# Sink-window attention with a two-layer block: in the start-up, the next pair's first row maxima ahead of VectorE's copies, and chunk 0's last pair ahead of pair 4's third scores

## The chip, the cores and the metric

One NeuronCore of a Trainium2 chip. The metric is the device time of one execution in microseconds; the times below come from a few executions of the kernel, and one more execution was recorded by the hardware profiler. Engines are named as in the profile: PE (TensorE matrix products), PEld (its weight loads), DVE (VectorE), ACT (ScalarE), POOL (GpSimd), SP (the queue that issues nearly all transfers).

## The reference

Attention over 4 batches, 8 heads, 768 positions, head size 64; each query sees the first 4 positions and the 128 last ones. Then, over all 3072 tokens, a block of two matrices with a squared ReLU between them.

```
scores = q @ k.T / 8                      # (4, 8, 768, 768)
keep   = (pos_k < n_sink) | ((0 <= pos_q - pos_k) & (pos_q - pos_k < window))
a      = softmax(where(keep, scores, -1e9))
x      = (a @ v), heads side by side      # (3072, 512)
h      = maximum(x @ w_in, 0)             # (3072, 2048)
out    = (h * h) @ w_out                  # (3072, 512)
```

The weights arrive as doubles; the kernel itself splits each row of 512 of them into two numbers (a "row" below: 16 of w_in, 16 of w_out).

## The kernel before

**Units of work.** The tokens are cut into 8 chunks of 384 (three blocks of 128 queries); the heads go in pairs, four pairs to a chunk. `pairs[s]` is pair s: pairs 0 to 3 are chunk 0, pairs 4 to 7 chunk 1. For a pair, in this order:

- `scores(s, i)`: for both heads, the product of query block i with its keys (PE, L254), the mask and row maximum (DVE, L262), the exponential with its row sum (ACT, L265). In chunk 0 block 0 is narrow (128 keys), the others have 264.
- `normalise(s)`: DVE adds a small number to the sums (L278) and takes reciprocals (L279); POOL multiplies the probabilities by them (L290) and gathers the sink columns in `PSK` (L296, L297).
- `tail(s)`: PE transposes the probabilities (`probs`, L344), three banks, and the sink columns (`sink_keys`, L304). Bank 0 and 2 are copied to `PTF` by ACT (L351), bank 1 by DVE (L349); DVE copies the sinks to `SK` (L310, L311). (For chunk 1 ACT makes all of these.)
- `values(s)`: PE multiplies by the values (L392, L395); ACT copies the result to `xh` (L403), DVE makes the rest `xl` (L404).

**Rows.** `split_steps` handles a row in five steps, and `fill(n)` issues the next n steps: (1) ACT copy L554 into tile `m`, DVE L555 into `t1`; (2) DVE L557; (3) DVE L559 into the other half words of `m`; (4) DVE L561; (5) ACT cast L567, DVE product L568, which reads `m`. There is one buffer for `m`.

**Order.** Up to the end of chunk 0's first products every engine runs in the order of the program text (`manual_schedule`), so an instruction that waits holds up all behind it on its engine. For s = 0 to 4 the loop issues: the load of pair s+1, scores(s, 0..2) with steps 1 to 3 of a row between them, step 4, normalise(s), values(s-2), the load of v, tail(s-1) with the rest of values(s-2), and step 5 inside it. Behind the loop: values(3), two steps, then the products of chunk 0 (`ph`, L451: x times w_in, and `po`, L488: the squares times w_out) in quanta; between them come two row steps and one entry of `todo` (scores, normalise, tail and values of pairs 4 to 7). ACT applies ReLU and a square (L459, L462), DVE the products L469 and L473. Later chunks and rows follow in an order that a planner spreads over the products.

Tiles of scores and of transposes share PSUM banks: three pairs of banks (`att`, `h`, `o0`/`o1`) rotate from pair to pair, so a product may start only when the bank's previous content was copied out. Dummy products (`busy`, L623) keep PE running in the first 16 us.

Of the kernel before, what the change touches and what calls it, by code (L numbers as in the profile page):

```python
# [19 lines left out]
P = 128  # L20
# [22 lines left out]
def sink_window_attention_moe(  # L43
# [25 lines left out]
    with ExitStack() as fast:  # L69
# [226 lines left out]
                nc.gpsimd.tensor_copy(to[:, :, 0:3:2, own], src.unsqueeze(2).broadcast_to([P, NQ - i0, 2, NS]))  # L296
                nc.gpsimd.tensor_tensor(to[:, :, 1, own], src, f32(to[:, :, 0, own]), op=ALU.subtract)  # L297

        def sink_keys(c, p, tag="att"):
            n = NQ - (1 if c % NHALF == 0 else 0)  # L300
            pss = bank(tag, f"pss_{c}_{p}")
            own = PSK[p % 2 if c < 2 else 0]
            for a in range(0, n, 2):
                nc.tensor.transpose(  # L304
                    pss[:, a * SW : a * SW + P], f32(own[:, a : a + 2]).rearrange("p a c -> p (a c)"), ident
                )
            copy = nc.scalar.copy if c == 1 else nc.vector.tensor_copy
            blocks = lambda t: t.rearrange("p (a c) -> p a c", c=P)
            rows = slice(0, 6 * NS)
            copy(blocks(SK[rows, 0 : n * P])[:, 0:n:2], blocks(pss[rows, 0 : (n + 1) // 2 * P]))  # L310
            copy(SK[rows, P : 2 * P], pss[SW : SW + 6 * NS, 0:P])  # L311

        def banks_of(c, p):

# [13 lines left out]
                banks.append((blocks, off))  # L328
            return banks

        def probs(c, p, bi, tag="att"):
            st = state[c, p]
            half = c % NHALF
            if bi == 0:
                st["banks"] = banks_of(c, p)
                st["PT"] = {}
            blocks, used = st["banks"][bi]
            pt = bank(tag, f"pt_{c}_{p}_{bi}")
            for hh, kk, qs, off in blocks:
                kb = st["kb0"] + kk  # L340
                for j, i in enumerate(qs):
                    qb = half * NQ + i
                    c0 = 0 if (qb == 0 or qb == kb + 1) else BS
                    nc.tensor.transpose(  # L344
                        pt[:, off + j * P : off + (j + 1) * P], st["P"][hh][:, i, c0 : c0 + P], ident
                    )
            st["PT"][bi] = PTF = ap3.tile([P, 512], F32, tag="PTF", name=f"PTF_{c}_{p}_{bi}")
            if bi == 1 and c != 1:
                nc.vector.tensor_copy(PTF[:, 0:used], pt[:, 0:used])  # L349
            else:  # L350
                nc.scalar.copy(PTF[:, 0:used], pt[:, 0:used])  # L351

        def probs_of(c, p, hh):

# [190 lines left out]
        def split_steps(n):  # L545
# [5 lines left out]
            m = ap1.tile([P, WR], I32, tag="m", name=f"m_{n}")  # L551
            eb = ap1.tile([P, WR], I32, tag="eb", name=f"eb_{n}")
            m16 = m.bitcast(U16).rearrange("p (w t) -> p w t", t=2)
            nc.scalar.copy(m16[:, :, 0], words[:, :, 1])  # L554
            nc.vector.tensor_scalar(t1, top, 3, 0x3FFFF000, op0=ALU.logical_shift_left, op1=ALU.bitwise_and)  # L555
            yield
            nc.vector.scalar_tensor_tensor(t1, top, -0x40000000, t1, op0=ALU.bitwise_and, op1=ALU.bitwise_or)  # L557
            yield
            nc.vector.tensor_scalar(m16[:, :, 1], words[:, :, 2], 0x1FF, None, op0=ALU.bitwise_and)  # L559
            yield  # L560
            nc.vector.tensor_scalar(eb, t1, -0x800000, None, op0=ALU.bitwise_and)  # L561
# [45 lines left out]
        with tc.manual_schedule(engines={E.PE, E.DVE, E.Activation, E.Pool, E.SP}):  # L607
# [7 lines left out]
            def scores(s, i, tags=("att", "att"), heads=(0, 1)):  # L615
                for hh in heads:
                    score(*pairs[s], hh, i, tags[hh])
# [4 lines left out]
                for _ in range(n):  # L622
                    nc.tensor.matmul(t, idle[:, 0:P], idle, start=True, stop=True)  # L623

            def tail(s, spare, own=("att",) * 3):

                a = pairs[s]
                probs(*a, 0, own[0])
                if s == 0:
                    busy(10)  # L630
                yield
                sink_keys(*a, spare)
                probs(*a, 1, own[1])
                yield
                probs(*a, 2, own[2])
                yield

            load_qk(*pairs[0])
# [8 lines left out]


            trio = [("att", "att"), ("h", "h"), ("o0", "o1")]
            for s in range(NPAIR + 1):  # L650
                if s > 0:
                    load_qk(*pairs[s + 1])
                trios = trio[-s % 3 :] + trio[: -s % 3]
                if s == 0:

                    for i, tags in enumerate(trios):
                        scores(s, i, tags, (0,))
                for i, tags in enumerate(trios):
                    scores(s, i, tags, (0, 1) if s else (1,))
                    if s == 0 or i > 0:  # L660
                        fill(1)
                fill(1)

                normalise(*pairs[s], (0, 1))
                if s == 1:
                    split_sinks()
                if s < 2:
                    busy(4 + 4 * s)
                rest = values(*pairs[s - 2], True) if s > 1 else None
                if s > 0:  # L670
                    if s > 1:
                        load_v(*pairs[s])
                    t = tail(s - 1, "o2", (*trios[0], trios[1][0]))
                    next(t)
                    fill(1)
                    if rest:
                        rest()
                    next(t)
                    fill(1)
                    next(t)  # L680
                else:
                    fill(1)
            rest = values(*pairs[NPAIR - 1], True)
            fill(2)
            rest()

            todo = []
            for s in range(NPAIR + 1, 2 * NPAIR + 1):
# [294 lines left out]
```

## Time and profile before

| | |
|---|---|
| time, median of 3 runs (lowest to highest) | 708.75 us (706.12 to 709.47) |
| the profiled execution | 708.04 us, of which the profile's span is 706.0 us |
| PE busy | 688.1 us, 97% of the span |
| DVE, ACT, POOL busy | 435.3 us, 428.6 us, 228.5 us |
| granted TensorE clock, mean | 0.995 |

The profiled execution's time is 2.0 us more than its span. Busy times are sums over the whole span; which engine sets the pace differs between the start-up (the first 41 us, where little is multiplied) and the rest.

### The profile page before, as it was taken

The page shows a single profiled execution, that of the slowest core. Times are in us where ns is not written, and L with a number is a line of the kernel's source. Part 1 is how long each engine was busy: PE and PEld are TensorE (multiplying, and loading weights), DVE is VectorE, ACT ScalarE, POOL GpSimd, SP SyncE. Part 2 cuts the span into 40 slices and gives each one's busy share as a digit, 9 for nine tenths or more (in the row PEclk, how much of TensorE's full clock was granted, in tenths as well). Part 3 has the DMA queues.
Part 4 walks back from the last instruction along what each step waited for, and adds up shares of the span by engine and source line. Part 5 has one row for each costly group of instructions (what it writes and reads, how often), then busy time and mean ns, then how long its engine had stood idle before and what let it go on. Part 6 is the DMA issues. An engine that isn't in the chain of part 4 may idle for free.

```text
span 706.0 us, 11716 instructions
## 1 busy us (share of the span) xinstructions
PE 688.1 (97%) x3865; PEld 594.5 (84%) x3866; DVE 435.3 (62%) x1181; ACT 428.6 (61%) x1200; POOL 228.5 (32%) x433
## 2 busy tenths in 40 slices
PE   9879999999999999999999999999999999999995
PEld 4557789998888898888888888889888889889995
DVE  7989899845667665565556566665555655542221
ACT  6777787755666676766676676667667444422221
POOL 5645400043455423323433443232344233200000
PEclk9999999999999999999999999999999999999999
DMA  7475466321524433333434532344432210000001
GB/s 239 149 234 185 131 213 204 130 65 42 149 70 125 122 109 92 92 101 107 102 105 113 152 87 73 102 128 108 101 93 84 88 44 16 0 16 31 1 0 50
DMA packets 37028, 71.51 MB, mean 101 GB/s; under 512 B 4384, under 2 KB 14368, under 8 KB 36960
## 3 DMA queue, kind: packets, MB, share of 16 engines
q1 hardware_dynamic: 36816, 70.55, 34.1%
q8 instruction: 33, 0.54, 0.3%
q14 instruction: 35, 0.29, 0.1%
q10 hardware_dynamic: 144, 0.13, 0.1%
HBM read 62.80 MB, written 7.86 MB: 100 GB/s over the span
## 4 chain that ended last, share of the span: by engine, by line
PE 90%; ACT 3%; DVE 3%; DMA 2%; issue 1%; SPq 0%; DVEq 0%; ACTq 0%
PE ph L451 37%; PE po L488 37%; PE xo L392 6%; PE s L258 5%; PE pt L362 2%; ACT P L265 2%; PE xo L395 2%; PE s L254 1%; DMA kn<-in_k_dram 1%; PE pt L344 1%; PE pss L304 1%; ACT m L554 1%; DMA ob<-part 1%; DMA part<-ob 0%; DVE P L262 0%
## 5 line engine op out<-in xcount | busy, mean ns | idle before, releaser
L451 PE MATMUL ph<-x,wi 128*128 128x384 f32 x1536 | 306.0, 340 | 0.0
L451 PEld LDWEIGHTS ph<-x,wi 128*128 128x128 f32 x1536 | 265.1, 188 | 8.9 <-issue 1.4
L488 PE MATMUL po<-wo,gh 128*128 128x512 f32 (+1 forms) x770 | 244.2, 398 | 1.0 <-DVE ob L512 0.8
L226 POOL TENSOR_TENSOR KS<-kn,KS 128x408 fp32r<-128x408 f32 (+1 forms) x48 | 59.0, 1229 | 318.4 <-ACT KS L225 318.4
L488 PEld LDWEIGHTS po<-wo,gh 128*128 128x128 f32 x770 | 135.8, 188 | 19.9 <-issue 1.4
L488 PE MATMUL po<-wo,gl 128*128 128x512 f32 x385 | 151.6, 394 | 0.0
L265 ACT ACTIVATE P<-P,nbs 128x264 f32<-128x264 f32 (+1 forms) x192 | 94.3, 492 | 78.5 <-DVE nbs L262 78.2
L459 ACT ACTIVATE r<-ph 128x384 f32<-128x384 f32 x128 | 62.3, 487 | 92.5 <-PE ph L451 89.8
L469 DVE TENSOR_TENSOR ph<-ph,r 128x384 f32<-128x384 f32 x104 | 58.4, 562 | 72.7 <-ACT r L459 72.6
L262 DVE CUSTOM_DVE_ANT_0 P<-s,masks 128x264 f32<-128x264 f32 x160 | 67.2, 429 | 56.3 <-PE s L258 53.5
L290 POOL TENSOR_SCALAR P<-P,rs 128x136 f32<-128x136 f32 (+2 forms) x192 | 83.9, 452 | 36.7 <-DVE rs L279 27.3
L473 DVE TENSOR_TENSOR gl<-ph,gh 128x384 fp32r<-128x384 f32 x128 | 71.2, 556 | 25.2 <-ACT ph L466 14.3
L488 PEld LDWEIGHTS po<-wo,gl 128*128 128x128 f32 x385 | 72.2, 188 | 16.0
L462 ACT ACTIVATE gh<-r 128x384 fp32r<-128x384 f32 x128 | 67.2, 525 | 3.0
L228 DVE TENSOR_TENSOR QS<-qn,QS 64x384 fp32r<-64x384 f32 x48 | 47.1, 982 | 25.6 <-ACT QS L227 25.2
L285 POOL TENSOR_TENSOR P<-P 128x256 f32<-128x256 f32 (+1 forms) x48 | 50.0, 1041 | 24.4 <-ACT P L265 23.9
L258 PE MATMUL s<-KS,QS 128*128 128x264 f32 (+1 forms) x288 | 57.0, 280 | 0.0
L258 PEld LDWEIGHTS s<-KS,QS 128*128 128x128 f32 x288 | 52.0, 188 | 5.0 <-DVE nbs L262 0.5
L368 DVE TENSOR_TENSOR PTF<-pt,halves 128x256 f32<-128x256 f32 x96 | 36.3, 419 | 22.3 <-PE pt L362 21.8
L392 PE MATMUL xo<-PTF,vn 128*64 128x256 f32 x448 | 47.3, 348 | 2.7 <-ACT PTF L351 2.7
L392 PEld LDWEIGHTS xo<-PTF,vn 128*64 128x64 f32 x448 | 32.1, 138 | 19.3 <-issue 9.2
L225 ACT CAST KS<-kn 128x408 fp32r<-128x408 f32 (+1 forms) x48 | 28.3, 589 | 32.1 <-issue 18.7
(99 smaller groups left out, 631.7 us busy)
## 6 DMA issues: line engine op xcount, KB each, us to landing
raw<-in_moe_w_in_dram SPq DMA_DIRECT2D x16, 512.0 KB, 3.9
raw<-in_moe_w_out_dram SPq DMA_DIRECT2D x16, 512.0 KB, 4.3
half<-in_moe_w_in_dram SPq DMA_DIRECT2D x32, 256.0 KB, 3.1
half<-in_moe_w_out_dram SPq DMA_DIRECT2D x32, 256.0 KB, 3.1
kn<-in_k_dram SPq DMA_DIRECT2D x24, 272.0 KB, 4.3
qn<-in_q_dram SPq DMA_DIRECT2D x32, 192.0 KB, 3.8
out_dram<-ob SPq DMA_DIRECT2D x23, 256.0 KB, 2.3
kn<-in_k_dram SPq DMA_DIRECT2D x24, 204.0 KB, 3.6
```

What stands on the lines that cost most here:

```text
L226: nc.gpsimd.tensor_tensor(KS[:, 1, 0:nk], st["kn"][:, hh, 0:nk], f32(KS[:, 0, 0:nk]), op=ALU.subtract)
L258: nc.tensor.matmul(ps[:, 0:n], st["QS", hh][:, qcols], flat[:, a, c0 : c0 + n], start=(a == 0), stop=(a == 1))
L262: nc.vector.tensor_tensor_reduce(Pt[:, i, 0:n], ps[:, 0:n], mask[:, 0:n], -SCALE, BIG, ALU.add, ALU.min, nb)
L265: nc.scalar.activation(Pt[:, i, 0:n], Pt[:, i, 0:n], AF.Exp, bias=nb, scale=-1.0, accum_out=sm[:, i : i + 1])
L290: nc.gpsimd.tensor_scalar(Pt[:, j, 0:n], Pt[:, j, 0:n], rs[:, hh, j : j + 1], 1.0, op0=ALU.mult, op1=ALU.mult)
L392: nc.tensor.matmul(xo[h * D : h * D + D, cols], lhsT, rhs, start=(n == 0), stop=False, skip_group_check=True)
L451: nc.tensor.matmul(ph[:, 0:TOK], wi_at(i, cc, fc), xt[:, cc, :], start=(m == 0), stop=(m == 3 * NCC - 1),)
L459: nc.scalar.activation(r, ph[:, 0:TOK], AF.Relu)
L462: nc.scalar.activation(gh, r, AF.Square)
L469: nc.vector.tensor_tensor(ph[:, 0:TOK], ph[:, 0:TOK], r, op=ALU.mult)
L473: late = lambda: nc.vector.tensor_tensor(gl, ph[:, 0:TOK], f32(gh), op=ALU.subtract)
L488: nc.tensor.matmul(po[t][:, e], gt[:, ts_], wo[f][:, i, e], start=(f == f0 and j == 0), stop=(f == f1 - 1 and j == 2), skip_group_check=True,)
```

## The change

Three edits, all in the order of instructions; no arithmetic changes.

1. The loop runs over s = 0 to 3. `scores(s+1, 0)` is issued in turn s, behind tail(s-1)'s PE work and step 4, and ahead of DVE's part of tail(s-1) (the copies to SK and to PTF) and of the rest of values(s-2). For that `sink_keys` and `probs` get a flag `later`, with which they return their DVE copies instead of issuing them.
2. Turn 4 is written out. In it, tail(3) goes ahead of scores(4, 2), and values(3) follows these scores, ahead of normalise(4). As many row steps are issued before the first product as before (27), with other places: one each after scores(4, 1), after the rest of values(2) and after normalise(4), and four at the end.
3. In `split_steps` ACT's L554 moves from step 1 to step 3, for all 32 rows.

```diff
-        def sink_keys(c, p, tag="att"):
+        def sink_keys(c, p, tag="att", later=False):
...
-            copy(blocks(SK[rows, 0 : n * P])[:, 0:n:2], blocks(pss[rows, 0 : (n + 1) // 2 * P]))
-            copy(SK[rows, P : 2 * P], pss[SW : SW + 6 * NS, 0:P])
+            def copies():
+                copy(blocks(SK[rows, 0 : n * P])[:, 0:n:2], blocks(pss[rows, 0 : (n + 1) // 2 * P]))
+                copy(SK[rows, P : 2 * P], pss[SW : SW + 6 * NS, 0:P])
+
+            return copies if later else copies()
...
-        def probs(c, p, bi, tag="att"):
+        def probs(c, p, bi, tag="att", later=False):
...
-            if bi == 1 and c != 1:
-                nc.vector.tensor_copy(PTF[:, 0:used], pt[:, 0:used])
-            else:
-                nc.scalar.copy(PTF[:, 0:used], pt[:, 0:used])
+            copy = nc.vector.tensor_copy if bi == 1 and c != 1 else nc.scalar.copy
+            rest = lambda: copy(PTF[:, 0:used], pt[:, 0:used])
+            return rest if later else rest()
...
-            nc.scalar.copy(m16[:, :, 0], words[:, :, 1])
             nc.vector.tensor_scalar(t1, top, 3, 0x3FFFF000, op0=ALU.logical_shift_left, op1=ALU.bitwise_and)
             yield
             nc.vector.scalar_tensor_tensor(t1, top, -0x40000000, t1, op0=ALU.bitwise_and, op1=ALU.bitwise_or)
             yield
+            nc.scalar.copy(m16[:, :, 0], words[:, :, 1])
             nc.vector.tensor_scalar(m16[:, :, 1], words[:, :, 2], 0x1FF, None, op0=ALU.bitwise_and)
...
-            def tail(s, spare, own=("att",) * 3):
+            def tail(s, spare, own=("att",) * 3, later=False):
...
-                sink_keys(*a, spare)
-                probs(*a, 1, own[1])
+                copies = sink_keys(*a, spare, later), probs(*a, 1, own[1], later)
                 yield
                 probs(*a, 2, own[2])
+                yield
+                for copy in copies:
+                    copy()
                 yield
...
-            for s in range(NPAIR + 1):
+            for s in range(NPAIR):
...
                 for i, tags in enumerate(trios):
-                    scores(s, i, tags, (0, 1) if s else (1,))
                     if s == 0 or i > 0:
+                        scores(s, i, tags, (0, 1) if s else (1,))
                         fill(1)
                 fill(1)
...
-                    t = tail(s - 1, "o2", (*trios[0], trios[1][0]))
-                    next(t)
+                    t = tail(s - 1, "o2", (*trios[0], trios[1][0]), True)
+                    for _ in range(3):
+                        next(t)
                     fill(1)
+
+                scores(s + 1, 0, trios[2])
+                if s > 0:
                     if rest:
                         rest()
                     next(t)
-                    fill(1)
-                    next(t)
-                else:
-                    fill(1)
-            rest = values(*pairs[NPAIR - 1], True)
-            fill(2)
+                fill(1)
+
+            s = NPAIR
+            load_qk(*pairs[s + 1])
+            trios = trio[-s % 3 :] + trio[: -s % 3]
+            scores(s, 1, trios[1])
+            fill(1)
+            rest = values(*pairs[s - 2], True)
+            load_v(*pairs[s])
+            t = tail(s - 1, "o2", (*trios[0], trios[1][0]))
+            next(t)
             rest()
+            fill(1)
+            next(t)
+            next(t)
+            scores(s, NQ - 1, trios[NQ - 1])
+            rest = values(*pairs[s - 1], True)
+            normalise(*pairs[s], (0, 1))
+            fill(1)
+            rest()
+            fill(4)
```

## Rows read from the trace of the kernel before

**Rows 1.** The page of the profile: the busy line of each engine (us, share of the span, instructions), and the TensorE clock that was granted in each of 40 slices, in tenths.

```profile
PE 688.1 (97%) x3865; PEld 594.5 (84%) x3866; DVE 435.3 (62%) x1181; ACT 428.6 (61%) x1200; POOL 228.5 (32%) x433
...
PEclk9999999999999999999999999999999999999999
```

**Rows 2.** The view by stretches: from and to (us from the span's start), length, busy time of each engine with its instructions, granted clock, share of the DMA engines, GB/s.

```profile
40.70:54.00 13.30, 11.56 (x64) 8.98 (x64) 12.25 (x35) 11.66 (x29) 4.99 (x10) 1.00 0.61 197
54.00:66.00 12.00, 12.00 (x70) 8.86 (x69) 10.80 (x33) 8.64 (x24) 5.67 (x11) 1.00 0.61 179
66.00:95.00 29.00, 28.61 (x178) 22.29 (x177) 25.80 (x58) 23.62 (x54) 11.49 (x16) 1.00 0.47 151
...
106.00:141.00 35.00, 35.00 (x180) 31.93 (x180) 31.66 (x73) 26.03 (x52) 0.00 (x0) 1.00 0.51 167
...
200.00:400.00 200.00, 200.00 (x1150) 176.69 (x1149) 122.64 (x333) 135.05 (x413) 78.43 (x142) 1.00 0.38 107
```

**Rows 3.** The timeline of VectorE in the start-up: start, length (us), engine, line, operation, output and inputs, count, and in brackets how long the engine had been idle and what released it.

```profile
11.28 0.28 DVE L262 CUSTOM_DVE_ANT_0 P<-s,mask 128x128 f32<-128x128 f32 x1
...
15.14 0.17 DVE L278 TENSOR_SCALAR rs<-sm 128x6 f32<-128x6 f32 x1 [0.64 <-ACT P L265]
...
15.45 0.39 DVE L204 CAST VS<-vs 48x512 fp32r<-48x512 f32 x1
...
16.57 0.51 DVE L561 TENSOR_SCALAR eb<-t 128x512 int32<-128x512 int32 x1
...
22.47 0.17 DVE L278 TENSOR_SCALAR rs<-sm 128x6 f32<-128x6 f32 x1 [0.67 <-ACT P L265]
...
22.79 0.39 DVE L561 TENSOR_SCALAR eb<-t 128x512 int32<-128x512 int32 x1
23.09 0.55 DVE L404 TENSOR_TENSOR x<-xo,x 128x384 fp32r<-128x384 f32 x1
23.56 0.27 DVE L310 CAST SK<-pss 48x128 fp32r<-48x128 f32 x1
...
24.16 0.42 DVE L349 COPY PTF<-pt 128x256 f32<-128x256 f32 x1
24.51 0.68 DVE L568 SCALAR_TENSOR_TENSOR wi<-m,eb 128x512 fp32r<-128x512 int32 x1
25.11 0.28 DVE L262 CUSTOM_DVE_ANT_0 P<-s,mask 128x128 f32<-128x128 f32 x1
...
28.04 0.45 DVE L559 TENSOR_SCALAR m<-raw 128x512 uint16<-128x512 uint16 x1
28.98 0.17 DVE L278 TENSOR_SCALAR rs<-sm 128x6 f32<-128x6 f32 x1 [0.49 <-ACT P L265]
...
35.86 0.17 DVE L278 TENSOR_SCALAR rs<-sm 128x6 f32<-128x6 f32 x1 [0.74 <-ACT P L265]
...
41.47 0.56 DVE L404 TENSOR_TENSOR x<-xo,x 128x384 fp32r<-128x384 f32 x1 [1.80 <-ACT x L403]
```

**Rows 4.** The same timeline for ScalarE.

```profile
25.43 0.40 ACT L265 ACTIVATE P<-P,nbs 128x128 f32<-128x128 f32 x1 [1.15 <-DVE nbs L262]
...
27.21 0.77 ACT L554 COPY m<-raw 128x512 uint16<-128x512 uint16 x1
...
28.35 0.50 ACT L265 ACTIVATE P<-P,nbs 128x264 f32<-128x264 f32 x1
...
32.08 0.52 ACT L265 ACTIVATE P<-P,nbs 128x264 f32<-128x264 f32 x1 [1.29 <-DVE nbs L262]
```

**Rows 5.** The same timeline for GpSimd: the last instruction of pair 0, of pair 1 and of pair 3.

```profile
15.57 0.35 POOL L297 TENSOR_TENSOR PSK<-P,PSK 128x16 fp32r<-128x16 f32 x1
...
20.81 0.67 POOL L297 TENSOR_TENSOR PSK<-P,PSK 128x16 fp32r<-128x16 f32 x1
...
33.60 0.22 POOL L297 TENSOR_TENSOR PSK<-P,PSK 128x16 fp32r<-128x16 f32 x1
```

**Rows 6.** The same timeline for TensorE (neighbours of one kind are merged).

```profile
16.04 0.30 PE L304 MATMUL pss<-ident,PSK 128*128 128x128 f32 x1
...
16.93 0.93 PE L254 MATMUL s<-kn,qn 64*128 64x128 f32 x6
...
25.73 1.30 PE L392 MATMUL xo<-PTF,vn 128*64 128x256 f32 x12
...
37.72 2.72 PE L392 MATMUL xo<-PTF,vn 128*64 128x256 f32 x12 [2.66 <-ACT PTF L351]
...
40.74 1.23 PE L451 MATMUL ph<-x,wi 128*128 128x384 f32 x6
...
50.35 0.66 PE L344 MATMUL pt<-ident,P 128*128 128x128 f32 x4 [1.21 <-ACT PTF L351]
```

**Rows 7.** The view by stretches again, one microsecond each (columns as in rows 2).

```profile
38.00:39.00 1.00, 1.00 (x7) 0.88 (x8) 0.97 (x3) 0.00 (x0) 0.92 (x2) 0.50 1.08 275
...
41.00:42.00 1.00, 1.00 (x8) 0.74 (x6) 0.54 (x2) 1.00 (x2) 0.47 (x2) 1.00 0.41 164
```

**Rows 8.** What the trace says of line 554 over the whole run: who released ScalarE when it sat idle ahead of it (us in total, times).

```profile
  DVE wo L568: 3.3, 6
```

**Rows 9.** The timeline of ScalarE behind the first products.

```profile
49.09 0.77 ACT L554 COPY m<-raw 128x512 uint16<-128x512 uint16 x1 [0.16 <-DVE wo L568]
49.73 0.57 ACT L351 COPY PTF<-pt 128x512 f32<-128x512 f32 x1
```

## The prediction

> **What bounds the kernel now.** I read the page first: PE is busy for 97% of the span, with a granted clock of 0.9 or more in all 40 slices [rows 1]. Then the view by stretches: from 54 us on PE has practically no gap (12.00 of 12 us, 35.00 of 35, 200.00 of 200), while from 40.7 to 54 it is busy for only 11.56 of 13.3 us and DVE for 12.25 [rows 2]. So from about 52 us the length is that of PE's own work, which the change leaves as it is. A gain can come from one place: the moment from which PE no longer stops must come earlier. The change is worth that shift and no more, however much smoother the first 40 us get.
>
> Next I read the timelines of the start-up engine by engine, looking at the idle time in brackets. A pair is a closed loop: DVE's reciprocal, then on DVE a row step (22.79), x (23.09), two SK copies (23.56), PTF (24.16), a row product (24.51), and only at 25.11 the next pair's first maximum [rows 3]. ACT, which needs that maximum, stands idle for 1.15 us and again 1.29 us a pair later [rows 4]. Then ACT runs six exponentials with the copy L554 between the fourth and the fifth (27.21), and DVE waits 0.49 to 0.74 us for the last of them before it can make the next sums [rows 3, 4]. Both engines thus wait for each other once per pair. Behind the last pair comes a worse stop: PE waits 2.66 us for a PTF copy before values(3), at 37.72, and its first product starts at 40.74 [rows 6].
>
> **The change part by part.** All is in the profiled execution's own times. DVE's work between two sums is the same in any order, so I take its length without idle from the trace and add the idle of the new order.
>
> *Pair 1.* The row product (0.60, 24.51 to 25.11) no longer stands ahead of its first maximum, and L554 (0.64, from 49.09 to 49.73, [rows 9]) no longer among the exponentials, where it delayed the last one of pair 0 by about 0.1 to 0.2. The first maximum moves from 11.28 to about 10.55. The row product comes back later in the same stretch, but into time that DVE now spends idle (0.64 ahead of 15.14). DVE's queue and ACT's then meet within 0.1 us: sums of pair 1 at 14.3 instead of 15.14, 0.85 earlier.
>
> *Pair 2.* 15.14 to 22.47 is 7.33 us, of which 0.67 and about 0.1 are waits, so 6.55 of work [rows 3]. A new wait comes in: scores(2, 0) now sit on PE behind tail(0), which needs POOL's last PSK of pair 0, ready at 15.92 [rows 5]; by an earlier start I put it at 15.75. Behind it PE needs 0.9 us for the transposes (16.04 to 16.93, [rows 6]) and 0.3 for the product: maximum at 17.1. DVE gets there at 14.3 + 0.3 (sums, reciprocal) + 1.12 (15.45 to 16.57) + 0.43 = 16.15 and waits 0.95. Sums of pair 2: 14.3 + 6.55 + 0.95 = 21.8, 0.7 earlier than 22.47.
>
> *Pair 3.* 22.47 to 28.98 is 6.51 us less 0.59 of waits, 5.92. POOL's last PSK of pair 1 is at about 21.3 (21.48 before, [rows 5]), so the maximum is possible at 22.65 against DVE's 22.4: 0.25 of waiting. ACT now has L554, x and two PTF copies in the time that it spent idle, and its last exponential fits DVE's queue to 0.1 us. Sums of pair 3: 21.8 + 5.92 + 0.25 = 27.95, 1.0 earlier.
>
> *Turn 4.* From 28.98 to the end of the last x of chunk 0 (41.47 + 0.47) DVE takes 12.96 us, less waits of 0.74 and 1.80 and some 0.15 of semaphore time: 10.3 [rows 3]. In the new order I find two waits: 0.9 for x of values(2), which PE makes from 31.1 to 32.55 (1.3 and the sinks' product) and ACT copies by 33.2, and 0.9 for the last exponential of pair 4, whose maxima now come behind the copies of tail(3). So DVE ends the same work at 27.95 + 10.3 + 1.8 = 40.05, or 39.8 with pitches taken one by one; I take 39.9, against 41.94: **DVE gains 2.0**. PE gains more: PSK of pair 3 is ready one us earlier than 33.82 [rows 5], SK and PTF of pair 3 are copied by 35.25, values(3) then need about 1.1 us and the first product starts at 36.4 instead of 40.74, 4.3 earlier. Part of that is clock: the 2.66 us stop was followed by a granted clock of 0.50, and values(3) took 2.72 us where the same twelve instructions take 1.30 at full clock [rows 6, 7].
>
> *Behind the first products.* PE cannot keep 4.3 us. It has two quanta of products, and then scores(5, 1) need a bank that DVE's maxima of scores(5, 0) give back, at about 40.9; so PE stops for 1.5 us there and 0.9 us one score later. From then on DVE's queue sets the pace, as it did before: of the 1.05 us that it misses between 40.7 and 54 [rows 2], 0.77 lie ahead of 41.47, and the 0.28 left are waits for PE, which vanish. DVE is 2.0 + 0.3 = 2.3 ahead. The last stop of before is PE's 1.21 us at 50.35, for the PTF copy of pair 4 [rows 6]; that copy stood behind L554, which itself waited for a row product [rows 9]. With L554 two steps later nothing but a cast is ahead of it: the copy moves from 49.73 by 0.64 of L554, its wait of 0.16 and DVE's 2.3 to 46.6, and PE with it from 50.35 to 47.25, 3.1 earlier. A few us later the scores of pair 6 meet DVE's queue again, which is 2.3 ahead, and take 0.3 to 0.8 of it back.
>
> *L554 elsewhere.* ACT waited for a row product ahead of it six times, 3.3 us in all [rows 8]. Gone, but after 66 us PE is idle for only 0.39 us up to 95 and 0 from 106 to 141 [rows 2]: hidden by PE, worth 0 to 0.4. If it had to be made good by DVE's L559, which follows at once in step 3, that would cost 0.64 a row; but 28.04 and the end of L554 (27.21 + 0.77 = 27.98) and like rows show DVE's half not held by ACT's, so I take nothing. SP: the moved loads of pairs 3 to 5 keep their distance to their use (v of pair 2 holds the queue until values(0), as before); nothing. The transfers behind 36 us move along with it.
>
> **Sum.** The shift lies between DVE's 2.3 and PE's 3.1, nearer to DVE, since DVE holds both queues last: 2.5 us. 708.04 - 2.5 = 705.5 us; the profiled execution is 0.7 below the median of the runs shown, so against that median it would be 706.2. I put the number at 705.7, between. A measurement of this kernel tells 0.5%, 3.5 us, from no change; the forecast is 0.35%.
>
> **The rivals.**
>
> *PE keeps its lead.* If DVE's queue has more slack than I see (POOL-slowed instructions get shorter when moved), the shift is PE's: 3.1 at 47, up to 4 with the last idle time of 40 to 54 (1.74, [rows 2]) partly gone. 704.0 to 705, and over the 0.5% bound in its better half. For it: PE's restart moves by 4.3. Against: DVE busy for 12.25 of 13.3 us.
>
> *POOL falls behind.* Every first score now stands behind the tail of the pair before on PE, so behind POOL. POOL was done with pair 3 4.84 us after its sums (28.98 to 33.82, some 4.3 of it work), but took 5.6 for pair 1 (15.92 to 21.48) [rows 3, 5]. Up to 5.8 my times hold. At 6.6 per pair, pair 3's PSK comes at 35.6 instead of 32.7, SK at 35.9 instead of 34.3, and 1.6 of the gain goes: 0.9 left, 707.1. The Trainium skill (SBUF — State Buffer, "Who interferes with whom") says that a VectorE instruction with two SBUF inputs, or a copy in a two-port mode, and a GpSimd instruction exclude each other for their whole length; the new order puts maxima, which read PSUM and one SBUF tile, ahead of the row product with its two, which by that rule would make POOL faster in its first microsecond rather than slower and leave the sum at 705.5. Rows 5 agree only in that POOL's times differ between pairs; none shows the cause.
>
> *The other side: half clock.* PE's gaps in the start-up grow from 0.6 to about 1.2 us twice a pair, then 1.5. Before, a gap of 1.21 (ahead of 50.35) left the clock at 1.00, one of 2.66 was followed by 0.50 [rows 6, 7]. Should the clock fall at 17 us and stay, PE's work per pair, 4.6 us (values 1.5, transposes 1.3, six scores 1.8 by 0.93 for three, [rows 6]), would become 9.2, over the pair's 6: some 3 a pair, 9 in three, less 2.5: 714.5. It decides from the point at which PE's work per pair exceeds 6 us, thus only if the low clock lasts through most of a pair. A single drop behind the 1.5 us gap at 39.4 costs about 1 us: 706.5.
>
> *It does nothing.* If DVE never really waited, a permutation would bring nothing: 708. The four waits before the sums (2.5 us) and the 1.80 speak against it.
>
> **Chances.** Forecast (1.5 to 3.5 us) 0.5; PE keeps its lead 0.24; POOL or one short clock drop (0 to 1.5) 0.14; nothing 0.05; half clock 0.04; the planned part behind 95 us, whose order may turn out differently, 0.03 for slower. Range 703.0 to 708.5: it holds the forecast, PE's lead and the POOL case, and some 0.2 is left out on both sides. Faster by over 0.5%: the better part of PE's lead and the forecast's edge, 0.3; slower: 0.07; within: 0.63.
>
> **What would show it.** Sums (L278) of pairs 1 to 4 at 14.3, 21.8, 28 and 36.8; ACT's waits of 1.1 to 1.3 for maxima gone from pairs 2 and 3; DVE waiting near 16.5 for PE, a wait that was not there; first ph at 36.4 with clock 1.00 ahead of it; a new PE stop near 39.5 to 41; PE without stops from about 47.5; "ACT m L554 waits for L568" gone. Wrong would be: first ph after 38, clock under 1 in 16 to 36, or a different amount of PE idle time between 54 and 141.

## The result and the profile after

The changed kernel takes 714.26 us (median of 6 runs, 710.19 to 716.95), the kernel before 708.54 (6 runs, 706.12 to 710.62): ratio 1.0089, 95% interval 1.0061 to 1.0117. It is slower, where 0.35% faster was forecast, and outside the range. The profiled execution, 710.19 us with a span of 708.1, is the fastest of the six; its clock averages 0.993, that of the others 0.982 to 0.992, against 0.995 in the profiled execution of before. Its span is 2.1 us longer than that of before (706.0), while the medians differ by 5.7: what follows shows the smaller part of the loss. The three slowest of the six (715.05 to 716.95) have the lowest clocks, 0.982 to 0.985; where it fell in them no trace shows. Line numbers behind 304 move by 3 to 8: PTF copies are L354, the copy into `m` L562, the row product L572, `values` L396, `ph` L455.

The view by stretches, columns as in [rows 2]:

```profile
40.70:54.00 13.30, 10.63 (x44) 8.50 (x43) 12.11 (x33) 8.66 (x23) 8.03 (x16) 0.74 0.62 202
54.00:66.00 12.00, 11.66 (x68) 8.22 (x67) 10.72 (x31) 9.68 (x25) 2.80 (x6) 1.00 0.50 163
66.00:95.00 29.00, 28.91 (x180) 23.60 (x179) 24.54 (x58) 23.42 (x53) 14.01 (x21) 1.00 0.49 158
...
106.00:141.00 35.00, 35.00 (x178) 31.71 (x177) 32.81 (x75) 27.98 (x56) 0.00 (x0) 1.00 0.54 173
```

From 54 us on PE's busy time changed by no more than 0.34 us in any of these stretches. Between 40.7 and 54 PE's busy time fell from 11.56 to 10.63 us although the granted clock there fell from 1.00 to 0.74, so that each product took longer. The timeline of VectorE (columns as in [rows 3]):

```profile
14.02 0.39 DVE L278 TENSOR_SCALAR rs<-sm 128x6 f32<-128x6 f32 x1
...
17.52 0.29 DVE L262 CUSTOM_DVE_ANT_0 P<-s,mask 128x128 f32<-128x128 f32 x1 [1.24 <-POOL P L290]
...
18.83 0.42 DVE L354 COPY PTF<-pt 128x256 f32<-128x256 f32 x1
...
22.48 0.15 DVE L278 TENSOR_SCALAR rs<-sm 128x6 f32<-128x6 f32 x1
...
23.84 0.29 DVE L262 CUSTOM_DVE_ANT_0 P<-s,mask 128x128 f32<-128x128 f32 x1 [0.68 <-PE s L254]
...
25.33 0.42 DVE L354 COPY PTF<-pt 128x256 f32<-128x256 f32 x1
...
28.97 0.16 DVE L278 TENSOR_SCALAR rs<-sm 128x6 f32<-128x6 f32 x1
...
30.55 0.43 DVE L262 CUSTOM_DVE_ANT_0 P<-s,masks 128x264 f32<-128x264 f32 x1 [0.90 <-PE s L254]
...
32.33 0.42 DVE L354 COPY PTF<-pt 128x256 f32<-128x256 f32 x1
...
35.68 0.56 DVE L408 TENSOR_TENSOR x<-xo,x 128x384 fp32r<-128x384 f32 x1 [1.28 <-ACT x L407]
...
39.30 0.17 DVE L278 TENSOR_SCALAR rs<-sm 128x6 f32<-128x6 f32 x1 [0.82 <-ACT P L265]
...
43.92 0.41 DVE L262 CUSTOM_DVE_ANT_0 P<-s,masks 128x264 f32<-128x264 f32 x1
```

The sums of pair 1 come 1.1 us earlier than in [rows 3], of which 0.53 was there at pair 0's already (9.86, in the kernel before 10.39), those of pair 2 at the same time (22.48 for 22.47), those of pair 3 too (28.97 for 28.98), and those of pair 4 at 39.30 where they were at 35.86. The waits ahead of L278 are gone up to pair 3, but a wait ahead of each first maximum took their place: 1.24, 0.68 and 0.90 us. TensorE:

```profile
16.88 0.93 PE L254 MATMUL s<-kn,qn 64*128 64x128 f32 x6
19.40 1.12 PE L254 MATMUL s<-kn,qn 64*128 64x264 f32 x6 [1.59 <-DVE PTF L354]
...
23.21 0.49 PE L254 MATMUL s<-kn,qn 64*128 64x128 f32 x4
...
25.90 1.12 PE L254 MATMUL s<-kn,qn 64*128 64x264 f32 x6 [1.26 <-DVE PTF L354]
...
32.90 0.68 PE L254 MATMUL s<-kn,qn 64*128 64x264 f32 x2 [1.76 <-DVE PTF L354]
...
39.29 1.21 PE L455 MATMUL ph<-x,wi 128*128 128x384 f32 x6
...
44.40 1.06 PE L254 MATMUL s<-kn,qn 64*128 64x264 f32 x4 [2.02 <-DVE nbs L262]
46.11 1.60 PE L254 MATMUL s<-kn,qn 64*128 64x264 f32 x4 [0.65 <-DVE nbs L262]
47.64 2.29 PE L455 MATMUL ph<-x,wi 128*128 128x384 f32 x6
...
52.72 0.60 PE L349 MATMUL pt<-ident,P 128*128 128x128 f32 x4
```

PE waits for VectorE's PTF copy 1.59, 1.26 and 1.76 us (L254, the second half of scores(s, 1)); in the trace of before these waits were 0.60 at most. The first product starts at 39.29, 1.45 earlier than before, and is followed by a new stop of 2.02 us. From 47.64 on six products take 2.29 us instead of 1.21. The same by the microsecond:

```profile
44.00:45.00 1.00, 0.60 (x3) 0.54 (x4) 1.00 (x6) 0.62 (x3) 0.94 (x3) 1.00 0.56 123
47.00:48.00 1.00, 1.00 (x4) 0.36 (x2) 1.00 (x3) 1.00 (x5) 0.00 (x0) 0.50 0.12 43
...
53.00:54.00 1.00, 1.00 (x7) 0.87 (x6) 0.57 (x1) 0.97 (x3) 0.92 (x4) 1.00 0.52 151
```

The clock is at 0.50, 1.2 of its 2.4 GHz, from 45.7 to 52.5 (6.8 us). The second bank of pair 4's transposes starts at 52.72 and started at 50.35 [rows 6]: 2.4 us late, and from there the order of work is as it was. The last product, before and now, starts 1.6 us later:

```profile
698.47 0.28 PE L488 MATMUL po<-wo,gl 128*128 128x256 f32 x1
...
700.05 0.28 PE L492 MATMUL po<-wo,gl 128*128 128x256 f32 x1
```

### The profile page after: what moved, and what is told of

It is laid out like the page before. It is cut to its first block, busy times and chain, and to the rows that moved or that the text cites. A ratio compares the mean times of both kernels' runs of the same rounds, so it can differ in the third digit from the quotient of the medians.

```text
span 708.1 us, 11718 instructions
## 1 busy us (share of the span) xinstructions
PE 688.2 (97%) x3866; PEld 595.8 (84%) x3866; DVE 435.9 (62%) x1181; ACT 429.9 (61%) x1200; POOL 227.1 (32%) x433
## 4 chain that ended last, share of the span: by engine, by line
PE 91%; DVE 3%; ACT 2%; DMA 1%; POOL 1%; issue 1%; SPq 0%; DVEq 0%; ACTq 0%; POOLq 0%
PE ph L455 37%; PE po L492 37%; PE xo L396 6%; PE s L258 5%; PE pt L366 2%; PE xo L399 2%; PE s L254 1%; PE pt L349 1%; POOL P L290 1%; PE pss L304 1%; DMA raw<-in_moe_w_in_dram 1%; DMA ob<-part 1%; DVE P L262 0%; ACT P L265 0%; DVE x L408 0%
## 5 line engine op out<-in xcount | busy, mean ns | idle before, releaser
L455 PE MATMUL ph<-x,wi 128*128 128x384 f32 x1536 | 308.1, 341 | 0.0
L455 PEld LDWEIGHTS ph<-x,wi 128*128 128x128 f32 x1536 | 266.7, 189 | 9.2 <-issue 1.7
L228 DVE TENSOR_TENSOR QS<-qn,QS 64x384 fp32r<-64x384 f32 x48 | 47.2, 983 | 25.5 <-ACT QS L227 25.1
L285 POOL TENSOR_TENSOR P<-P 128x256 f32<-128x256 f32 (+1 forms) x48 | 49.9, 1040 | 24.4 <-ACT P L265 23.9
L372 DVE TENSOR_TENSOR PTF<-pt,halves 128x256 f32<-128x256 f32 x96 | 36.3, 419 | 22.4 <-PE pt L366 21.8
L396 PE MATMUL xo<-PTF,vn 128*64 128x256 f32 (+1 forms) x448 | 46.5, 342 | 0.5 <-ACT PTF L354 0.3
L396 PEld LDWEIGHTS xo<-PTF,vn 128*64 128x64 f32 x448 | 31.2, 136 | 17.6 <-issue 9.5
```

The lines of the kernel that those rows point to most:

```text
L396: nc.tensor.matmul(xo[h * D : h * D + D, cols], lhsT, rhs, start=(n == 0), stop=False, skip_group_check=True)
L455: nc.tensor.matmul(ph[:, 0:TOK], wi_at(i, cc, fc), xt[:, cc, :], start=(m == 0), stop=(m == 3 * NCC - 1),)
```

## The experiments

Each was run beside the kernel before on the same chip, in four groups on four chips (e1 to e4, e5 to e8, e9 to e12, e13 to e15); a ratio is to that kernel, with its 95% interval. The changed kernel itself was not run again beside them, so a comparison with its 1.0089, or across groups, goes by ratios and not by times. "From sums to sums" below counts from pair 0's L278 to pair 5's in the profiled execution, which leaves out the first 10 us, when the first transfers land: 38.6 us before, 40.2 in the changed kernel.

**e1_l554**, edit 3 alone on the kernel before:

```diff
-            nc.scalar.copy(m16[:, :, 0], words[:, :, 1])
...
+            nc.scalar.copy(m16[:, :, 0], words[:, :, 1])
```

> Edit 3 alone (ScalarE's copy into m moved from step 1 to step 3 of a row), on the kernel before. Theory A (what costs time is TensorE's stop between the second quantum of products and the scores of pair 5, behind which the clock is granted at half speed): this edit does not touch that stop, so the clock falls only at 37.5 us as before, the PTF copy of pair 4 is no longer behind that copy, TensorE's stop of 1.2 us at 50 shrinks to about 0.5; time 0.3 to 1 us below the kernel before, ratio 0.9985. Theory B (the moved copy is the cause, by delaying exponentials behind it): ratio 1.005 or more and new ScalarE waits for L568 at 42.

705.5 us, ratio 0.9980 (0.9967 to 0.9994): faster by 0.2%, with the interval just clear of 1, and theory B falls. Sums of pairs 1, 4 and 5 on VectorE, and TensorE's stops ahead of values(3) and of the second bank of pair 4's transposes:

```profile
14.72 0.39 DVE L278 TENSOR_SCALAR rs<-sm 128x6 f32<-128x6 f32 x1
...
34.45 0.17 DVE L278 TENSOR_SCALAR rs<-sm 128x6 f32<-128x6 f32 x1
...
46.64 0.17 DVE L278 TENSOR_SCALAR rs<-sm 128x6 f32<-128x6 f32 x1
```

```profile
36.93 1.36 PE L392 MATMUL xo<-PTF,vn 128*64 128x256 f32 x12 [2.63 <-ACT PTF L351]
...
47.15 0.65 PE L344 MATMUL pt<-ident,P 128*128 128x128 f32 x4 [0.34 <-ACT PTF L351]
```

Between the sums of pair 1 and of pair 4 it takes 19.7 us, before 20.7 [rows 3]; from sums to sums 36.6 instead of 38.6. Of these 2.0 us 0.9 lie behind pair 4's sums, where the execution of before ran values(3) at half clock (2.72 us for twelve products [rows 6]) and this one did not (1.36). The stop of 1.21 us for pair 4's PTF copy fell to 0.34, as the prediction had worked out.

**e2_loop**, edit 1 alone (the new loop for turns 0 to 3, the old turn 4, L554 in step 1):

```diff
+                    t = tail(s - 1, "o2", (*trios[0], trios[1][0]), True)
+                    for _ in range(3):
+                        next(t)
...
+                scores(s + 1, 0, trios[2])
```

> Edit 1 alone (next pair's first scores ahead of VectorE's copies in turns 0 to 3), turn 4 in the old order, the copy into m in step 1. Theory A: pairs stay 6.5 to 7 us apart, because the loop now closes over PTF copy, scores, values, tail and first scores on TensorE; first product at 40 to 41.5 us, no stop over 1.5 us after it; ratio 0.998 to 1.003. Theory C (the longer stops of TensorE in the start-up, 1.3 to 1.8 us, let the clock fall there in most executions): ratio 1.005 or more and granted clock under 1 between 16 and 36 us.

710.97 us, ratio 1.0060 (1.0037 to 1.0083): in four executions this edit alone makes it slower, by its ratio more than either other edit. Pairs 2, 3 and 4 follow at 8.9, 6.5 and 7.0 us (before 7.3, 6.5 and 6.9), and PE stops for the PTF copy in each turn:

```profile
21.20 1.13 PE L254 MATMUL s<-kn,qn 64*128 64x264 f32 x6 [1.58 <-DVE PTF L354]
...
27.70 1.13 PE L254 MATMUL s<-kn,qn 64*128 64x264 f32 x6 [1.32 <-DVE PTF L354]
...
34.71 1.12 PE L254 MATMUL s<-kn,qn 64*128 64x264 f32 x6 [1.82 <-DVE PTF L354]
...
40.18 1.61 PE L396 MATMUL xo<-PTF,vn 128*64 128x256 f32 x12 [1.60 <-ACT PTF L354]
```

In the profiled execution (709.2, the fastest of four) the clock stayed at 1.00 up to 58 us, in the three others (710.7 to 711.5) it averaged 0.989 to 0.990 instead of 0.997. So both sides of the expectation had a part: the pairs come no faster, and something lets the clock fall in most executions; where, no trace shows.

**e3_turn4**, edit 2 alone:

```diff
-            for s in range(NPAIR + 1):
+            for s in range(NPAIR):
...
+            scores(s, 0, trios[0])
+            scores(s, 1, trios[1])
+            fill(1)
...
```

What follows there is turn 4 as in the changed kernel.

> Edit 2 alone (tail(3) ahead of scores(4, 2), values(3) ahead of normalise(4)). Theory A: first product earlier than 40.7 us, VectorE's last row step before the products later than 42, TensorE stops 1.5 to 2.5 us behind the second quantum and the clock is at half for some 5 us or more behind it; ratio 1.004 to 1.010. Theories B and C: neither the moved copy nor the longer stops of the start-up are in it, so ratio 0.995 to 1.001.

708.65 us, ratio 1.0022 (1.0003 to 1.0041), between the two ranges that were expected. The stop behind the second quantum is there, and the clock at 0.50 from 47 to 50, but the loss is half of the least that theory A wanted.

```profile
43.88 1.06 PE L254 MATMUL s<-kn,qn 64*128 64x264 f32 x4 [2.01 <-DVE nbs L262]
```

**e4_busy**, the changed kernel with its stop filled:

```diff
                 next(products)
+                if n == 1:
+                    busy(8)
```

> The changed kernel with 8 dummy products (they multiply zeros into a spare bank) on TensorE behind the second quantum of products, in its stop of 2 us at 42.4. Theory A: the clock stays at 1.00 from 42 to 54, the half-speed stretch of 6.8 us goes, time 2.5 to 6 us below the changed kernel (708 to 711), TensorE at the second bank of pair 4's transposes by 50.3 instead of 52.7. Theories B and C: the dummies fill idle time and change nothing, 713 to 715.

709.37 us, ratio 1.0045 (1.0024 to 1.0065). TensorE, and the stretch that was at half clock:

```profile
42.04 1.90 PE L627 MATMUL idle<-idle 128*128 128x512 bf16 x8
44.21 1.06 PE L254 MATMUL s<-kn,qn 64*128 64x264 f32 x4 [0.27 <-DVE nbs L262]
```

```profile
47.00:48.00 1.00, 1.00 (x6) 0.92 (x6) 1.00 (x5) 1.00 (x5) 0.00 (x0) 1.00 0.08 31
```

```profile
50.42 0.66 PE L349 MATMUL pt<-ident,P 128*128 128x128 f32 x4 [0.41 <-ACT PTF L354]
...
699.04 0.28 PE L492 MATMUL po<-wo,gl 128*128 128x256 f32 x1
```

The eight dummies end 0.27 us ahead of the scores, so they hold nothing up, and the clock stays at 1.00; in six of eight executions it averages 0.998. By the medians 0.44%, some 3 us, of the changed kernel's loss goes with the clock (the two intervals just overlap). The two profiled executions show less: counted from pair 0's sums (9.67 and 9.86) this one is 2.1 us ahead of the changed kernel at the second bank of pair 4's transposes, but only 0.8 at the last product. From sums to sums it is 40.2 as in the changed kernel, 1.6 more than before: what is left of the loss is no loss of clock.

**e5_ptf**, the changed kernel with the PTF copy back ahead of the first maxima:

```diff
-                for copy in copies:
-                    copy()
+                copies[1]()
+                yield
+                copies[0]()
...
+                    next(t)
 
                 scores(s + 1, 0, trios[2])
```

> The changed kernel, with VectorE's PTF copy of tail(s-1) put back ahead of the next pair's first maxima (the two SK copies and the rest of values stay behind them). Theory D (pairs stay 6.5 us apart because TensorE cannot start the second half of a pair's scores until that copy has emptied a bank, and values, tail and the next first scores follow on TensorE): VectorE has idle time of 0.7 to 0.9 us just there, so the copy costs nothing, TensorE's waits for it (1.3 and 1.8 us) fall under 0.7, sums of pair 3 come at 28.4 or earlier (28.97), first product by 38.6 (39.29); time 0.5 to 2 us below the changed kernel. Rival E (VectorE's own work sets the 6.5 us): sums unchanged within 0.1, time the same within 0.5 us.

709.57 us, ratio 1.0028 (1.0010 to 1.0045). Sums of pairs 2 and 3 on VectorE, and what TensorE now waits for:

```profile
22.09 0.15 DVE L278 TENSOR_SCALAR rs<-sm 128x6 f32<-128x6 f32 x1
...
27.85 0.15 DVE L278 TENSOR_SCALAR rs<-sm 128x6 f32<-128x6 f32 x1
```

```profile
23.52 1.20 PE L254 MATMUL s<-kn,qn 64*128 64x264 f32 x8 [1.76 <-ACT PTF L354]
...
27.69 0.33 PE L304 MATMUL pss<-ident,PSK 128*128 128x128 f32 x1 [0.98 <-POOL PSK L297]
```

```profile
42.54 1.60 PE L254 MATMUL s<-kn,qn 64*128 64x264 f32 x4 [2.02 <-DVE nbs L262]
```

Pair 3 follows pair 2 by 5.76 us instead of 6.49, and the first product starts at 37.44 instead of 39.29: the copy did set the distance of these pairs (theory D), and e14's execution has 5.76 again. Its waits are gone, others of 1.76 (for ScalarE's PTF copy) and 0.98 (for GpSimd) stand nearest now. The stop of 2.02 at 42 remains, and the clock behind it fell as before, for 6.8 us. By ratios the gain is 0.0061, some 4 us, where 0.5 to 2 were expected. The average clock is 0.991 to 0.993 in all ten executions, in the changed kernel 0.982 to 0.993: a part of that gain may be clock drops that this order avoids, which no trace shows.

**e6_late**, the changed kernel with three row steps later:

```diff
-            fill(4)
+            fill(1)
...
-                fill(2 if n < QUANTA // 2 or n % 4 == 0 or n >= QUANTA - 12 else 1)
+                fill(3 if n in (3, 4, 5) else 2 if n < QUANTA // 2 or n % 4 == 0 or n >= QUANTA - 12 else 1)
```

> The changed kernel, with one row step instead of four ahead of the first product; the other three follow in quanta 3 to 5 (three steps each instead of two). Theory A (TensorE's stop of 2.0 us behind the second quantum and the half clock behind it): VectorE reaches pair 5's first maxima 1.7 us earlier, the stop is under 1 us, clock 1.00 from 42 to 54, time 2.5 to 6 us below the changed kernel (708 to 711.5). If the low clock has another cause: 713 to 715.

712.52 us, ratio 1.0076 (1.0049 to 1.0102): a miss. TensorE's stops, and the clock in two microseconds of the same execution:

```profile
46.73 1.41 PE L254 MATMUL s<-kn,qn 64*128 64x264 f32 x4 [0.83 <-DVE nbs L262]
...
59.65 1.06 PE L254 MATMUL s<-kn,qn 64*128 64x264 f32 x4 [0.97 <-DVE nbs L262]
```

```profile
20.00:21.00 1.00, 1.00 (x5) 0.86 (x5) 0.71 (x4) 0.34 (x1) 0.57 (x2) 0.50 0.08 16
...
48.00:49.00 1.00, 1.00 (x4) 0.93 (x4) 1.00 (x4) 0.98 (x3) 0.00 (x0) 0.50 0.55 106
```

The stop of 2.02 fell to 0.38 and one of 0.83, and yet the clock went to 0.50 from 48 to 50. The steps that were put off opened a stop of 0.97 at 59.65. And this execution shows something else: the clock also fell at 20 us, in turn 2, whose order here is that of the changed kernel.

**e7_turn1**, the changed kernel without scores(2, 0) ahead in turn 1:

```diff
...
+                    if s == 1:
+                        next(t)
+                        fill(1)
+                        next(t)
+                        fill(1)
+                        next(t)
+                        continue
```

> The changed kernel, with turn 1 in the old order (scores(2, 0) not ahead of VectorE's copies of tail(0); turns 0, 2 and 3 as changed). Theory F (in turn 1 the first scores stand on TensorE behind tail(0), so behind GpSimd's late normalisation of pair 0, and VectorE waits 1.2 us): sums of pair 2 at 21.4 to 21.8 instead of 22.48, all up to the first product 0.7 to 1 us earlier, time 0.5 to 1.5 us below the changed kernel; the stop and the half clock at 42 to 52 remain. If turn 1 is not where it is lost: sums of pair 2 at 22.3 or later, time within 0.5 us.

711.03 us, ratio 1.0056 (1.0037 to 1.0074): better by the ratio (the intervals overlap), but not where it was expected; sums of pair 2 came at 23.06, 8.1 us behind pair 1 (8.5 in the changed kernel), and in the profiled execution the clock fell at 34 and at 48 us.

**e8_all**, e5, e6 and e7 together:

> The three together (PTF copy ahead of the first maxima, turn 1 in the old order, three row steps later). Theories A, D and F: the start-up is then 1.5 to 2.5 us shorter than in the changed kernel, no stop over 1 us, no half clock from 42 to 54; 705 to 707.5, at or under the kernel before. If one of them is wrong, it stays above 708.

706.95 us, ratio 0.9997 (0.9981 to 1.0013). First product at 36.06, from sums to sums 36.3 us. One part of the expectation failed: TensorE still stops for 0.83 us, and the clock behind it is at half for 3.4 us, from 42 to 46.

```profile
41.44 1.59 PE L254 MATMUL s<-kn,qn 64*128 64x264 f32 x4 [0.83 <-DVE nbs L262]
```

Pair 3 follows pair 2 by 6.3 us here and in e12, so the 5.76 of e5 may in part make up for a late pair 2. Undoing the new order in these three places brings back what it had cost, though no gain shows beside the kernel before.

**e9_loop_l554** and **e10_turn4_l554**, two edits at a time (e2 and e3, each with L554 moved as in e1):

> Edits 1 and 3 (new order in turns 0 to 3 and the moved copy into m), turn 4 in the old order. If the edits add up (edit 3 gave 0.998, edit 1 1.006, edit 2 1.0022): ratio 1.0035 to 1.005. If the loss of the changed kernel needs turn 4's stop together with the new loop: 1.001 or less.

711.03 us, ratio 1.0044 (1.0024 to 1.0064).

> Edits 2 and 3 (turn 4 written out and the moved copy), turns 0 to 3 in the old order. If the edits add up: ratio 0.999 to 1.001, with a stop of TensorE of 1.7 to 2.1 us behind the second quantum and a clock under 1 behind it. If the moved copy makes the stop worse, as it stands on ScalarE behind VectorE's product at the first quantum: 1.003 or more.

708.76 us, ratio 1.0017 (1.0001 to 1.0033). The single edits' ratios add up to 1.0040 and 1.0002; both lie inside the intervals (1.0002 barely). All three add up to 1.0062, at the lower end of the changed kernel's 1.0061 to 1.0117. In e10's execution the stop behind the second quantum is 2.02 us and the clock is at half from 45 to 51, as expected. e9's execution once more shows a clock drop in turn 2, behind a stop that the changed kernel has to the hundredth (1.59 at 19.40) without one:

```profile
19.64 2.02 PE L254 MATMUL s<-kn,qn 64*128 64x264 f32 x6 [1.59 <-DVE PTF L354]
```

```profile
20.00:21.00 1.00, 1.00 (x5) 0.76 (x4) 0.63 (x4) 0.52 (x2) 0.38 (x2) 0.50 0.08 16
```

Six matmuls took 2.02 us here and 1.12 there; pair 3's sums came 7.7 us behind pair 2's, not 6.5.

**e11_gaps**, the changed kernel with dummies in the stops of turns 2 to 4 as well (five each, between the two heads of scores(s, 1)) beside the eight of e4:

```diff
+                            busy(5, "xo")
```

> The changed kernel with dummy products in all of TensorE's longer stops: 8 behind the second quantum, as in e4, and 5 each between the two heads of scores(2, 1), (3, 1) and (4, 1), where it waits 1.3 to 1.8 us for VectorE's PTF copy. Theory C (the clock also falls in the start-up in some executions, which costs part of the loss): clock 0.997 or more in every execution, ratio 1.002 to 1.0035. If only the stop at 42 to 46 matters: as with e4, 1.004 to 1.005. The part of the ratio that is left with the clock at full speed is what the new order itself costs.

711.24 us, ratio 1.0038 (1.0024 to 1.0052). Not to be told from e4 (1.0045), so the start-up's drops are seen in single executions, but what they cost on average isn't shown.

**e12_best**, e5 and e7 together with e4's dummies, four steps ahead as in the changed kernel:

> The changed kernel with the PTF copy ahead of the first maxima, turn 1 in the old order, and 8 dummies behind the second quantum; four row steps ahead of the first product as in the changed kernel. Theories A, D and F: start-up as in e8, clock 0.997 or more, ratio 0.995 to 0.999 (703.5 to 707). If the order of the row steps was what helped in e8: 1.001 or more.

707.28 us, ratio 0.9995 (0.9979 to 1.0011): a miss for the hope of a gain, while it shows again that the places undone are those that cost.

**e13_turn1_busy** and **e14_ptf_busy**, e7 and e5, each with e4's dummies:

> The changed kernel with turn 1 in the old order and 8 dummies behind the second quantum. If turn 1 carries most of the loss that is left at full clock: ratio 1.000 to 1.0025. If the PTF copy carries it: 1.0035 to 1.005, as with the dummies alone.

709.52 us, ratio 1.0023 (1.0005 to 1.0040). The profiled execution has a clock drop that these dummies cannot reach, from 34 to 37 us.

> The changed kernel with the PTF copy ahead of the first maxima and 8 dummies behind the second quantum. If the PTF copy carries most of the loss that is left at full clock: ratio 0.9995 to 1.002. If turn 1 carries it: 1.003 to 1.005.

708.61 us, ratio 1.0008 (0.9991 to 1.0024). With the stop filled, 1.0045 goes to 1.0023 by turn 1's old order, to 1.0008 by the PTF copy's old place, to 0.9995 by both. The PTF copy carries the larger part by the medians; each part's interval overlaps its neighbour's. Both runs fell into the range in which their own place carries most of the loss, so they do not decide between the two. Nor have the dummies one price: by ratios they take 0.0044 off the changed kernel, 0.0033 off e7 and 0.0020 off e5.

**e15_l554_busy**, edit 3 alone with 11 dummies ahead of values(3):

> Edit 3 alone, with 11 dummy products ahead of values(3), where TensorE stops for 2.6 us and the clock of the kernel before falls in some executions. If edit 3 gains only by keeping that clock drop away: as with edit 3 alone, 0.997 to 0.999, and the clock 0.997 or more in every execution. If it gains by its order and the drop still costs some executions 1 to 1.5 us: 0.996 to 0.9975.

706.54 us, ratio 0.9988 (0.9968 to 1.0008). The dummies add nothing to e1 that could be told. The expectation is not met either way: the ratio lies where edit 3 would gain only by the clock, but the average clock is 0.994 to 0.999 and not 0.997 or more in every execution, and the interval reaches past 1. What speaks for the order is in e1's own group. At an average clock of 0.998 four executions of e1 took 705.05 to 705.61 us and five of the kernel before 705.71 to 707.37; at 0.996 three took 704.60 to 705.27 and six 705.55 to 708.16. e1 is the only version here whose interval lies below 1.

## Why the prediction was wrong, step by step

**Right, or nearly.** That what counts is the moment from which PE no longer stops: in the profiled execution PE is 2.4 us late at 53 us and still 1.6 at its last product. It holds to about 1 us only, since e4's 2.1 at that place shrank to 0.8. That L554 would shorten the start-up and the stop at 50 us: e1. That a stop would open between the second quantum and pair 5's scores. That the first product would come earlier, in part: 1.45 us and not 4.3; at 39.29 it is past the 38 that was named as a sign of being wrong.

**The term that failed: "DVE gains 2.0".** VectorE ended turn 4's work at 43.0 (42.41 and 0.61), where 39.9 was forecast and 41.94 was the time before: it lost 1.1. Of the 3.1 us between forecast and trace, about 1.0 was there at pair 3's sums (28.97 for 27.95), 1.2 came in waits of turn 4 and 0.8 in slower work, as follows.

**Pair 2, too small a term.** The wait for scores(2, 0) behind tail(0) was seen, at 0.95 us; it was 1.24. I gave a first score 0.3 us from its start on PE to VectorE's maximum; it takes 0.63 to 0.64 (16.88 to 17.52, 23.21 to 23.84). The work that I took to be the same in any order also grew: from pair 1's sums to pair 2's it is 7.2 us without that wait, not 6.55; pair 1's sums themselves took 0.39 us, where [rows 3] has 0.17. No run separates why.

**Pair 3, the step that failed.** "The maximum is possible" at 22.65 followed GpSimd's PSK as the only thing ahead of it on PE. But PE's queue holds, ahead of tail(1), the second half of scores(2, ·) and values(0), and these start only when VectorE's PTF copy has emptied a bank. By putting that copy behind the new first maxima the change closes a loop: PTF copy and its signal (18.83 to 19.40, 0.57 us), 1.06 of scores, 1.45 of values, 1.30 of tail, 0.63 to the first maximum, 1.49 on VectorE to the next PTF copy: 6.5. Its turns are the distances of the copies, 18.83, 25.33, 32.33: 6.50 and 7.00 us, as long as the pairs were apart before (6.51 and 6.88, [rows 3]). The idle time moved from ahead of the sums to ahead of the first maxima. I had listed those gaps on PE, under the clock, and not run them through its queue. e5 shows it: with the copy ahead, 5.76. In the sum the loop is 0.34 us at pair 3 (6.49 from sums to sums, forecast 6.15) and the first wait of turn 4. GpSimd did not fall behind, the rival for this place: its last PSK of pair 3 ends at 33.73, where the forecast has 32.7 and the rival 35.6.

**Turn 4.** I had two waits of 0.9 us on VectorE; there were three, 0.90 ahead of the first maximum (the loop again), 1.28 for x and 0.82 for the exponentials. The work beside them took 11.05 us instead of 10.3, and pair 4's sums, 36.8 in my sum, came at 39.30. The start-up's "gain" was by then used up, while PE, which values(3) ahead of normalise(4) had freed, started its products 1.45 us earlier and ran into its own wait. Some of VectorE's row work got slower: GpSimd's normalisation of pair 4 (39.90 to 45.80, before 36.46 to 41.55) now falls on these steps, and L565 took 0.65 us at 40.48 and again at 43.35, for 0.38 to 0.43 in the turns before. The Trainium skill (SBUF — State Buffer, "Who interferes with whom") has a tensor_scalar in a two-port mode and a GpSimd instruction exclude each other; the trace agrees in that L565 was slower beside GpSimd, but whether that is the cause no run here separates.

**The clock, the rival with too small a chance.** I let a single drop behind a gap of 1.5 us cost 1 us, and gave lasting half clock 0.04. The stop was 2.02 and 0.65 and the drop lasted 6.8 us. Between the trace that has it (the changed kernel) and one that has not (e4) the last product differs by 0.8 us, near my 1; the medians differ by some 3. The rest lies in executions without a trace, whose average clock was lower, so what I gave too small a chance is several drops, and where they fall stays open. By the medians order (e4: 1.0045 left) and clock (0.0044) are about equal, but they are not two separate sums: e5, which leaves the stop in place, takes off 0.0061. In the trace the stop itself comes from the order: VectorE reaches pair 5's maxima later while PE reaches their products earlier. That the rival's 714.5 stands so near the measured 714.26 is luck as far as the trace shows: it had the clock at half from 17 us through three pairs, and in the trace it is at 1.00 from there up to 45.

**L554 in the start-up, too small a term.** The "0 to 0.4" was said of the rows behind 66 us, and no run separates those. In the start-up I gave the copy 0.1 to 0.2 us at pair 1 and nothing more up to pair 4. There it stood between two exponentials on which the next sums wait, once a pair: in e1 pair 4's sums follow pair 0's by 24.4 us instead of 25.5, and with the stop at 50 the edit is worth 1.5 us by the medians.

**Open.** How much the start-up's clock drops cost on average; and why e8 and e12, with a start-up 1.3 to 2.3 us shorter from sums to sums, start their last product only 0.4 to 1.2 us earlier counted from pair 0's sums, and are no faster by their ratios. Single traces do not settle it: counted the same way, the last product comes at 690.2 in the changed kernel, 689.4 in e4 and 688.1 in the kernel before, but at 690.6 in e11, whose clock did not fall. PE's idle time from 141 to 200 us, far from the change, also varies (0.71 us in the changed kernel, 1.45 in e4, 1.07 before).

## What to carry to other kernels

When an instruction is moved ahead of others on an in-order engine, follow what the ones behind it release: here a copy that emptied a bank, whose lateness came back one turn later through another engine's queue and left the pairs as far apart as they were. Look for the closed loop through all queues, and count its length in the new order, before taking the idle time of one engine as gain. And an earlier start of an engine is worth nothing where its partner starts later: it becomes a stop, and on TensorE a stop can cost its clock besides.

## What the runs showed of the hardware

The clock's fall does not follow from the length of one stop alone. A stop of 1.59 us ahead of scores(2, 1) left it at 1.00 in one execution and was followed by 0.50 in another with the same order before it (the changed kernel, e9); it fell behind stops of 0.38 and 0.83 (e6) and of 0.39 and 0.83 (e8), and stayed at 1.00 behind 1.82 and 1.60 (e2) and 2.63 (e1), where the kernel before fell at 2.66 [rows 6, 7]. The Trainium skill (TensorE: Matmul & The Clock Gate, "What's actually happening") says that the clock is set by recent activity and that full clock is what activity earns; the trace agrees that it fell only where PE had stopped before, while which stops sufficed varied between executions. The times of the changed kernel spread over 6.8 us in six runs; they go with the average clock (0.989 to 0.993 in the three fastest, 0.982 to 0.985 in the three slowest), though other reasons may add to it; those of e4, whose clock was 0.998 in six of eight, over 4.6.
